# A fused attention and MLP kernel: work of its front end moved between ScalarE, VectorE and GpSimd, steps of two blocks at other places, one weight block fewer resident

## The chip, the cores and the metric

The kernel runs on one core of a Trainium2 chip. The core has a matrix engine (TensorE, PE in the profile), VectorE (DVE), ScalarE (ACT), GpSimd (POOL), SyncE (SP), which here only issues DMAs, and 16 DMA engines. The engines run side by side; each takes its own instructions in order and waits on semaphores for the others. On-chip data lies in SBUF, results of TensorE in eight banks of PSUM. The metric is the device time of one execution in microseconds, median over several runs. A profiled execution has a time and a trace of its own.

## The reference

Eight batches of 576 tokens go through attention with pooled keys and values (8 heads of 64), then through a Fourier mixing step, a layer norm and an MLP. The core of it:

```python
k_p = k.reshape(B, H, Sp, pool, D).mean(axis=3)        # Sp = 72, pool = 8
v_p = v.reshape(B, H, Sp, pool, D).mean(axis=3)
scores = scale * np.matmul(q, k_p.transpose(0, 1, 3, 2))
scores = scores - np.max(scores, axis=-1, keepdims=True)
attn = np.exp(scores)
attn = attn / (np.sum(attn, axis=-1, keepdims=True) + 1e-09)
x = np.matmul(attn, v_p)                # heads side by side: 8 x 576 x 512
...
mixed = np.real(fft(fft(x, axis=1), axis=2))
u = x + mixed
un = (u - mean(u)) / np.sqrt(var(u) + 1e-06)
out = u + np.maximum(un @ w_ch1, 0.0) @ w_ch2          # 512 -> 2048 -> 512
```

The factor on the scores is 1/8 for the head size, and the sum over 8 pooled keys needs another 1/8: together the 1/64 of the title's first part.

## The kernel before

**Split numbers.** TensorE multiplies numbers of type fp32r, which hold fewer bits than f32. Wherever accuracy is needed an operand is split into a high part (rounded to fp32r) and a low part (what is left), and a product becomes three: high by high, high by low, low by high. In names an h or "high" stands for the first, an l or "low" for the second. A high part is a cast, mostly on ScalarE; a low part is a subtraction, on VectorE or GpSimd.

**Two streams.** The MLP works on 9 blocks of 512 tokens (k = 0 to 8). Blocks 0 and 1 are plain: 12 matmuls of 128x512 make one tile of the hidden layer (line 875, tile g), and 12 more put it through the second weight matrix into four accumulators (line 839, tiles acc). Blocks 2 to 8 are the fast form: seven products of 128x256 (line 943, tile x) for a pair of tiles, joined by VectorE (adds L904, copy L947), a relu and a cast on ScalarE (L912, L913) and a subtraction on GpSimd (L914), and then the same line 839. Each block needs its tokens from a front end, fe(b) for batch b, which is made while the blocks before it run:

- scores of queries and pooled keys (psS, L422) with kpb, the pooled keys as written by the copies L360 and L361; row maxima; for b >= 2 a small VectorE multiplication of the maxima by 1/64 (L427); exp on ScalarE with scale 1/64 (L431); normalization on GpSimd (L439);
- V weights: sums over 8 on GpSimd (L352), the high part wh by ScalarE with a mask (L390), the low part wlo by VectorE (L391), for b >= 2; then transposes T, V and R of the attention (L459 to L483) and the product (psX, L507);
- the Fourier step: even and odd sums (tmpE L598, tmpO), their split (L591 on ScalarE, L592 on VectorE), and matmuls with cosine and sine tables (psA L631, psB L648, psQ and psP L665);
- means (psM), centring (L748), squares, variance (psVar, L792) and 1/sqrt; for b = 0 and 1 the result is spread over the partitions by a diagonal matrix dg (VectorE, L807 and L808) and a matmul into the same PSUM bank (L810); for b >= 2 the tokens X are multiplied by it in two halves of 128x1152, one on VectorE and one on GpSimd (L819), then split for the fast products (L723).

**Weights.** The two weight matrices arrive as 32 blocks of f64 (512 KB each). prep_w makes an f32 from each on ScalarE and VectorE (L191, L193, L195, L196), a high part on ScalarE (L203) and a low part on GpSimd (L205), and writes both to DRAM. The first ten are made before the first large matmul, beside the front end of batch 0; the others follow at every third step of blocks 0 and 1. RES lists the W2 high blocks that stay in SBUF; the others are read again for each block of tokens by SP's queue, nine tiles ahead (feed, LOOK).

**What sets the order.** fast() is a generator that yields after each group of matmuls; its count is the position pos. At each position, advance(pos) calls the next step of a front end if the tables say so: AT1 for fe(1), AT2 for fe(2), AT for the rest, each a list of positions, one per step. From position 92 on TensorE's order is as written; the other engines' order is left to a scheduler that simulates them, with VectorE's instructions of the fast products at high priority. issue_after holds an instruction behind a named one in that order (behind[...]). After block 0 four PSUM banks are shared by all tiles of front end and products; the other four are accumulators.

## Time and profile before

| quantity | value |
|---|---|
| median of 3 runs | 1103.25 us (1102.32 to 1977.59) |
| the profiled execution | 1107.79 us, of which the trace spans 1105.9 us |
| mean granted TensorE clock | 0.96 |
| ScalarE busy | 545.4 us (49%) |
| GpSimd busy | 543.6 us (49%) |
| instructions in the trace: TensorE, VectorE, ScalarE, GpSimd | 5974, 1442, 1607, 518 |
| largest DMA queue, share of 16 engines | 70.9% |
| TensorE's clock by slices of 27.6 us, the first ten, in tenths | 8 8 8 7 9 9 9 8 8 9 |

How it is read. A row names the source line, the engine, the operation and the program's tiles as out<-in. A wait in TensorE's list is idle time of TensorE, put down to the instruction that ended last before it could go on. A group's mean hides how it spreads, so where an engine's single instructions matter the timeline is read instead: start, duration, engine and line, with the idle time and its releaser in brackets behind. TensorE runs at a clock that the chip grants it, in tenths of full speed in the slices and as a number in the rows of a window; a low number means that the same matmuls take longer. The span is 1.9 us shorter than the time of the profiled execution, and that time is 4.5 us above the median.

### The profile page before, as it was taken

To read this page: it belongs to the slowest core of one execution; us is meant where nothing else is said; L and a number is where in the kernel's file an instruction comes from. 1 tells how busy PE (TensorE), PEld (TensorE's weight loads), DVE (VectorE), ACT (ScalarE), POOL (GpSimd) and SP (SyncE) were. 2 spreads that over 40 slices of the span, in tenths; PEclk is the share of its full clock that TensorE was granted. 3 is DMA by queue.
4 is the path that set the end of the run, shared out by engine and by line. 5 is a ranking of instruction groups with operands and counts; after the bars stand their busy time and mean duration, and the time that the engine had idled before them with its cause. 6 is when DMAs were issued, how large, how long until landed. Compare 5 with 4: busy or idle time off the path is not lost.

```text
span 1105.9 us, 18798 instructions
## 1 busy us (share of the span) xinstructions
PE 1017.3 (92%) x5974; PEld 878.2 (79%) x5974; DVE 747.4 (68%) x1442; ACT 545.4 (49%) x1607; POOL 543.6 (49%) x518
## 2 busy tenths in 40 slices
...
GB/s 297 230 188 347 274 318 262 208 220 262 207 141 127 196 223 209 211 262 220 197 227 194 255 207 224 222 243 223 206 191 235 198 197 243 306 256 254 302 253 144
DMA packets 160162, 253.75 MB, mean 229 GB/s; under 512 B 15808, under 2 KB 73152, under 8 KB 159808
## 3 DMA queue, kind: packets, MB, share of 16 engines
q1 hardware_dynamic: 159776, 249.88, 70.9%
q0 software_dynamic: 288, 2.66, 0.6%
q8 instruction: 49, 0.80, 0.3%
q14 instruction: 49, 0.40, 0.1%
...
## 4 chain that ended last, share of the span: by engine, by line
PE 64%; DVE 17%; DMA 6%; ACT 6%; issue 4%; POOL 3%; SPq 0%; DVEq 0%; ACTq 0%; POOLq 0%
PE acc L839 27%; PE x L943 20%; PE g L875 4%; PE psX L507 2%; PE psS L422 2%; PE psA L631 2%; DMA sx<-w1d 2%; PE psP L665 2%; PE psB L648 1%; DMA w1s<-sx 1%; DVE wlo L391 1%; DVE X L819 1%; DVE sx L904 1%; PE psQ L665 1%; DVE rw L400 1%
## 5 line engine op out<-in xcount | busy, mean ns | idle before, releaser
L914 POOL TENSOR_TENSOR hl<-sx,hh 128x512 fp32r<-128x512 f32 x112 | 151.7, 1354 | 217.7 <-ACT hh L913 198.0
L904 DVE TENSOR_TENSOR sx<-x,sx 128x256 f32<-128x256 f32 x336 | 155.3, 465 | 129.7 <-PE x L943 126.7
L943 PE MATMUL x<-un0h,w1op 128*128 128x256 f32 x896 | 176.0, 283 | 4.9 <-ACT U L510 1.5
L839 PE MATMUL acc<-hh,w2low 128*128 128x512 f32 x576 | 164.7, 399 | 0.0
L912 ACT ACTIVATE sx<-sx 128x512 f32<-128x512 f32 x112 | 71.2, 636 | 184.9 <-DVE sx L904 184.5
L943 PEld LDWEIGHTS x<-un0h,w1op 128*128 128x128 f32 x896 | 144.2, 191 | 16.5 <-DVE X L748 1.8
L943 PE MATMUL x<-un1h,w1op 128*128 128x256 f32 x672 | 134.0, 281 | 0.2
L943 PEld LDWEIGHTS x<-un1h,w1op 128*128 128x128 f32 x672 | 111.7, 189 | 13.4 <-DVE sx L904 1.5
L839 PEld LDWEIGHTS acc<-hh,w2low 128*128 128x128 f32 x576 | 101.6, 190 | 15.9
L839 PE MATMUL acc<-hh,w2high 128*128 128x512 f32 x324 | 98.3, 411 | 10.4 <-ACT hh L913 10.4
L839 PE MATMUL acc<-hl,w2high 128*128 128x512 f32 x324 | 94.5, 400 | 2.2 <-POOL hl L914 2.2
L943 PE MATMUL x<-un0l,w1op 128*128 128x256 f32 x448 | 88.8, 280 | 3.5 <-DVE un0l L723 3.5
L431 ACT ACTIVATE t<-psS,mx 128x72 f32<-128x72 f32 x240 | 73.5, 326 | 30.7 <-DVE mx L427 27.2
L439 POOL TENSOR_TENSOR t<-t,sm 128x720 f32<-128x720 f32 x30 | 45.8, 1526 | 64.0 <-DVE sm L438 47.5
L839 PEld LDWEIGHTS acc<-hh,w2high 128*128 128x128 f32 x324 | 58.8, 196 | 20.0 <-ACT hh L913 11.2
L839 PE MATMUL acc<-hl,w2h 128*128 128x512 f32 x252 | 72.2, 408 | 0.5 <-DVE hl L881 0.5
L943 PEld LDWEIGHTS x<-un0l,w1op 128*128 128x128 f32 x448 | 68.7, 190 | 3.7 <-DVE un0l L723 3.7
L913 ACT CAST hh<-sx 128x512 fp32r<-128x512 f32 x112 | 69.6, 621 | 2.9
L839 PE MATMUL acc<-hh,w2h 128*128 128x512 f32 x252 | 70.0, 398 | 1.0 <-DVE U L863 0.9
L839 PEld LDWEIGHTS acc<-hl,w2high 128*128 128x128 f32 x324 | 57.2, 189 | 12.2 <-POOL hl L914 3.2
L943 PE MATMUL x<-un1l,w1op 128*128 128x256 f32 x336 | 66.0, 278 | 0.0
L352 POOL TENSOR_TENSOR v<-v 128x256 f32<-128x256 f32 (+1 forms) x56 | 52.2, 931 | 26.1 <-DMA v<-in_vm 25.3
...
## 6 DMA issues: line engine op xcount, KB each, us to landing
...
w1op<-w1p SPq DMA_DIRECT2D x200, 256.0 KB, 3.6
w2low<-w2l SPq DMA_DIRECT2D x128, 256.0 KB, 3.4
...
```

The lines of the kernel that those rows point to most:

```text
L352: nc.gpsimd.tensor_tensor(out=out if n == 1 else src[:, :, 0:n], in0=src[:, :, 0] if n == 1 else src[:, :, 0:n], in1=src[:, :, 1] if n == ...
L422: nc.tensor.matmul(ps[:, c * W2J:(c + 1) * W2J], lhsT=q[:, r0:r0 + P], rhs=kpb[g % 2], start=True, stop=True)
L431: behind["S", b, gi, i] = nc.scalar.activation(t[:, c0 + c, h], pv[:, c, h], AF.Exp, scale=1.0 / 64.0, bias=mx[x], accum_out=sm[x])
L439: ins = nc.gpsimd.tensor_tensor(out=t, in0=t, in1=sm.unsqueeze(3).broadcast_to([P, 5, 2, J]), op=ALU.mult)
L665: nc.tensor.matmul(ps, lhsT=w, rhs=a, start=(i == 0), stop=(i == 6))
L839: nc.tensor.matmul(acc[e], lhsT=a[:, e], rhs=h, start=(f == 0 and x == 0), stop=(f == NFC - 1 and x == 2))
L875: nc.tensor.matmul(ps, lhsT=w[:, c], rhs=x[:, ti], start=(n == 0), stop=(n == 11))
L904: nc.vector.tensor_tensor(out=o, in0=x, in1=y, op=ALU.add)
L912: nc.scalar.activation(c, c, AF.Relu)
L913: nc.scalar.copy(out=h, in_=c)
L914: nc.gpsimd.tensor_tensor(out=l, in0=c, in1=raw(h), op=ALU.subtract)
L943: nc.tensor.matmul(ps, lhsT=w[:, q, i], rhs=y[:, c + i], start=(n == 0), stop=(n == 5))
```

## The change

Six edits and their tables:

1. K: the copies that write kpb multiply by 1/64; the multiplication of the maxima (L427) goes, and exp loses its scale.
2. V weights: ScalarE writes the masked f32 values to a new tile wf, casts it whole to wh, and GpSimd makes wlo by one subtraction of 128x128. The VectorE instructions L391 go (batches 0 and 1 are as before).
3. Tokens, b >= 2: four VectorE multiplications of 128x576 take the place of a VectorE and a GpSimd one of 128x1152.
4. Low weights: the subtraction L205 moves from GpSimd to VectorE for all 32 blocks.
5. Two splits in halves: L592 (b >= 2) and the centring L748 become two instructions each.
6. Order: the sign step L195 of weight blocks 0 to 3 is held behind the last low part of batch 0's psB (behind["Bv", 0]). AT1 and AT2 have other positions: AT2's come one or two earlier from its 18th entry on, AT1's last five 4 to 7 later or as they were. RES has six blocks where it had seven.

```diff
-RES = [0, 2, 5, 7, 9, 12, 14]
+RES = [0, 3, 6, 9, 11, 14]
...
-AT1 = [-1] * 7 + [2 + 3.5 * n for n in range(17)] + [93, 101, 106, 109, 112, 112, 112]
+AT1 = [-1] * 7 + [2 + 3.5 * n for n in range(17)] + [93, 101, 113, 116, 117, 117, 117]
...
-            nc.vector.tensor_scalar(out=dh[:, :, :, 1], in0=halves[:, :, :, 3], scalar1=0x8000, scalar2=None, op0=ALU.bitwise_and)
+            with tc.issue_after(behind["Bv", 0].ins) if n < 4 else ExitStack():
+                nc.vector.tensor_scalar(out=dh[:, :, :, 1], in0=halves[:, :, :, 3], scalar1=0x8000, scalar2=None, op0=ALU.bitwise_and)
...
-        nc.gpsimd.tensor_tensor(out=lw, in0=d0, in1=raw(wh), op=ALU.subtract)
+        nc.vector.tensor_tensor(out=lw, in0=d0, in1=raw(wh), op=ALU.subtract)
...
-                nc.scalar.copy(out=kb[0:64, 0:J], in_=ks[0:64])
-                nc.scalar.copy(out=kb[64:128, J:W2J], in_=ks[64:128])
+                nc.scalar.mul(kb[0:64, 0:J], ks[0:64], 1.0 / 64.0)
+                nc.scalar.mul(kb[64:128, J:W2J], ks[64:128], 1.0 / 64.0)
...
+            wf = wk.tile([P, P], F32, tag="wf", bufs=2, name="wf")
             for m, c, n, s0 in cols:
-                mm = mk[:, m:m + 1]
-                nc.scalar.mul(wh[:, c:c + n], vs[:, s0:s0 + n], mm)
-                nc.vector.scalar_tensor_tensor(out=wl[:, c:c + n], in0=vs[:, s0:s0 + n], scalar=mm, in1=raw(wh[:, c:c + n]), op0=ALU.mult, op1=ALU.subtract)
+                nc.scalar.mul(wf[:, c:c + n], vs[:, s0:s0 + n], mk[:, m:m + 1])
+            nc.scalar.copy(out=wh, in_=wf)
+            nc.gpsimd.tensor_tensor(out=wl, in0=wf, in1=raw(wh), op=ALU.subtract)
...
-                    nm = mx[:, c0:c0 + n]
-                    nc.vector.tensor_scalar(out=nm, in0=nm, scalar1=1.0 / 64.0, scalar2=None, op0=ALU.mult)
...
-                            behind["S", b, gi, i] = nc.scalar.activation(t[:, c0 + c, h], pv[:, c, h], AF.Exp, scale=1.0 / 64.0, bias=mx[x], accum_out=sm[x])
+                            behind["S", b, gi, i] = nc.scalar.activation(t[:, c0 + c, h], pv[:, c, h], AF.Exp, bias=mx[x], accum_out=sm[x])
...
-            eng.tensor_tensor(out=el, in0=src, in1=raw(eh), op=ALU.subtract)
+            for x in [slice(0, 2)] if b < 2 else [slice(0, 1), slice(1, 2)]:
+                eng.tensor_tensor(out=el[:, x], in0=src[:, x], in1=raw(eh[:, x]), op=ALU.subtract)
...
-            nc.vector.tensor_tensor(out=dst[0][:, n:2 * n], in0=ps, in1=raw(dst[0][:, 0:n]), op=ALU.subtract)
+            behind["Bv", b] = nc.vector.tensor_tensor(out=dst[0][:, n:2 * n], in0=ps, in1=raw(dst[0][:, 0:n]), op=ALU.subtract)
...
-            nc.vector.tensor_tensor(out=X[:, :, cl], in0=Ub[:, :, cl], in1=ps.unsqueeze(1).broadcast_to([P, 4, HS]), op=ALU.subtract)
+            for x in (0, 2):
+                nc.vector.tensor_tensor(out=X[:, x:x + 2, cl], in0=Ub[:, x:x + 2, cl], in1=ps.unsqueeze(1).broadcast_to([P, 2, HS]), op=ALU.subtract)
...
-            for e, x in ((nc.vector, slice(0, 2)), (nc.gpsimd, slice(2, 4))):
-                e.tensor_tensor(out=X[:, x], in0=X[:, x], in1=rn.unsqueeze(1).broadcast_to([P, 2, S]), op=ALU.mult)
+            for x in range(4):
+                nc.vector.tensor_tensor(out=X[:, x], in0=X[:, x], in1=rn, op=ALU.mult)
```

In the new file the lines stand one or two further down: L205 is L206, the cast to wh and GpSimd's subtraction are L392 and L393, L592 is L593, L748 L749, L810 L812, L819 L821, L839 L841, L875 L877, L904 L906, L913 L915, L947 L949.

By count, VectorE loses 60 L391, 48 L427 and the six old halves of L819, and gains 32 low weights, 24 token steps, 12 halves of L592 and 16 of L748. GpSimd loses 32 low weights and six token halves and gains 24 subtractions of 128x128. ScalarE gains 24 casts of 128x128. TensorE has the same matmuls. SP has eight more reads of a W2 block and one more write.

Three places of the order, before and after. First TensorE, in block 1, around the steps of fe(1) that AT1 places: the variance matmul L792 and the one that spreads 1/sqrt, L810, from the name psVar and the operand dg. Before:

```order
L792 MATMUL psVar_2097<-avg,lf 128x1 x5
L875 MATMUL g_1_2_2118<-un0h_869,w1op 128x512 x4
L875 MATMUL g_1_2_2118<-un0l_870,w1op 128x512 x4
L875 MATMUL g_1_2_2118<-un0h_869,w1op 128x512 x4
L839 MATMUL acc_0_2072<-hh,w2h 128x512
...
L839 MATMUL acc_3_2075<-hh,w2low 128x512
L810 MATMUL psVar_2097<-dg,avg 128x288 x2
```

After, the rows that end at the same matmul, now L812:

```order
L841 MATMUL acc_2_2076<-hl,w2high 128x512
L841 MATMUL acc_3_2077<-hl,w2high 128x512
L877 MATMUL g_1_3_2203<-un0h_871,w1op 128x512 x4
L471 MATMUL psV_0_2208<-ident,t_3_1881 128x128
L471 MATMUL psV_0_2208<-ident,t_2_1970 128x128
L472 MATMUL psV_0_2208<-ident,rt 32x128
L877 MATMUL g_1_3_2203<-un0l_872,w1op 128x512 x4
L483 MATMUL psR_0_2224<-ident,rt 32x128 x4
L877 MATMUL g_1_3_2203<-un0h_871,w1op 128x512 x4
L812 MATMUL psVar_2099<-dg,avg 128x288 x2
L424 MATMUL psS_0_0_2253<-kpb_78,q_0_2046 128x144 x3
```

L810 came 20 large matmuls behind L792 (rows of the two are left out above); L812 comes 48 behind, with transposes of fe(2) (psT, psV, psR) ahead of it too.

Second VectorE, in a block from the third on, at the token scaling (X<-X,rb) and the copy L947 that TensorE's products need (sx<-x). Before:

```order
L464 TENSOR_TENSOR al<-psT_2_6152,ah 128x512
L786 SCALAR_TENSOR_TENSOR nt<-nt,lf 128x576
L904 TENSOR_TENSOR sx<-x,sx 128x256
L478 TENSOR_TENSOR al<-psV_0_6190,ah 128x64
L787 SCALAR_TENSOR_TENSOR rb<-nt,lf 128x576
L478 TENSOR_TENSOR al<-psV_0_6190,ah 128x64
L819 TENSOR_TENSOR X<-X,rb 128x1152
L947 COPY sx<-x 128x256
L491 TENSOR_TENSOR R<-psR_0_6204,R 32x512
L491 TENSOR_TENSOR R<-psV_0_6190,R 32x64
```

After:

```order
L464 TENSOR_TENSOR al<-psT_2_6160,ah 128x512
L788 SCALAR_TENSOR_TENSOR nt<-nt,lf 128x576
L906 TENSOR_TENSOR sx<-x,sx 128x256
L478 TENSOR_TENSOR al<-psV_0_6196,ah 128x64
L789 SCALAR_TENSOR_TENSOR rb<-nt,lf 128x576
L478 TENSOR_TENSOR al<-psV_0_6196,ah 128x64
L821 TENSOR_TENSOR X<-X,rb 128x576 x2
L949 COPY sx<-x 128x256
L821 TENSOR_TENSOR X<-X,rb 128x576 x2
L491 TENSOR_TENSOR R<-psR_0_6210,R 32x512
L491 TENSOR_TENSOR R<-psV_0_6196,R 32x64
```

The copy stood behind one step of 128x1152 and stands behind two of 128x576, with two more after it.

Third VectorE, in a later batch, at the V weights (wlo, rw) and the sums and split of the Fourier step (tmpE, f), with the adds of the fast products (sx<-x) between them. Before:

```order
L391 SCALAR_TENSOR_TENSOR wlo<-vs,mk,wh 128x64
L904 TENSOR_TENSOR sx<-x,sx 128x256
L518 TENSOR_TENSOR U_85<-psX_1_5296,U_85 128x288
L598 TENSOR_TENSOR tmpE<-U_85 128x2x287
L391 SCALAR_TENSOR_TENSOR wlo<-vs,mk,wh 128x63
L391 SCALAR_TENSOR_TENSOR wlo<-vs,mk,wh 128x1
L400 SCALAR_TENSOR_TENSOR rw_81<-vt,mk,rw_81 32x63
L400 SCALAR_TENSOR_TENSOR rw_81<-vt,mk,rw_81 32x1
L904 TENSOR_TENSOR sx<-x,sx 128x256
L592 TENSOR_TENSOR f<-tmpE,f 128x580
L904 TENSOR_TENSOR sx<-x,sx 128x256
L904 TENSOR_TENSOR sx<-x,sx 128x512
```

After:

```order
L517 TENSOR_TENSOR U_85<-psX_1_5302,U_85 128x288
L518 TENSOR_TENSOR U_85<-psX_1_5302,U_85 128x288
L906 TENSOR_TENSOR sx<-x,sx 128x256
L599 TENSOR_TENSOR tmpE<-U_85 128x2x287
L402 SCALAR_TENSOR_TENSOR rw_81<-vt,mk,rw_81 32x63
L402 SCALAR_TENSOR_TENSOR rw_81<-vt,mk,rw_81 32x1
L609 TENSOR_TENSOR xe<-xt,xe 1x290
L906 TENSOR_TENSOR sx<-x,sx 128x256
L593 TENSOR_TENSOR f<-tmpE,f 128x290 x2
L906 TENSOR_TENSOR sx<-x,sx 128x256
L906 TENSOR_TENSOR sx<-x,sx 128x512
```

The three rows of wlo are gone, and the split of f is two halves, which stand together.

6 lines of the change are left out of this document (3 added, 3 removed).

## The prediction

> **What bounds the kernel now.** I read the page's first part and its chain, then TensorE's own waits, then the timelines around the longest of those waits, then windows for the granted clock.
>
> ```profile
> PE 1017.3 (92%) x5974; PEld 878.2 (79%) x5974; DVE 747.4 (68%) x1442; ACT 545.4 (49%) x1607; POOL 543.6 (49%) x518
> PE 64%; DVE 17%; DMA 6%; ACT 6%; issue 4%; POOL 3%; SPq 0%; DVEq 0%; ACTq 0%; POOLq 0%
> ```
>
> TensorE is busy for 1017.3 of 1105.9 us and holds 64% of the chain; VectorE holds 17% of it at 68% busy. Both programs have the same count of matmuls, so the change can only win what TensorE idles (88.6 us) and what it loses at a lower clock. The waits say who ends that idle time (us in total, times, longest):
>
> ```profile
> PE acc L839 <- ACT hh L913: 10.4, 4, 2.7
> PE psS L422 <- DVE sx L947: 9.9, 4, 2.5
> PE psVar L810 <- DVE dg L807: 7.8, 2, 6.7
> PE psA L631 <- DVE f L592: 4.1, 1, 4.1
> PE x L943 <- DVE un0l L723: 3.5, 1, 3.5
> ```
>
> Two waits of about 2.5 us come four times each, all from 340 us on; one of 6.7 us comes once. First the rows ahead of one "psS <- L947" wait (start, duration, engine):
>
> ```profile
> 345.75 1.36 DVE L819 TENSOR_TENSOR X<-X,rb 128x1152 f32<-128x1152 f32 x1
> ...
> 578.84 2.66 POOL L819 TENSOR_TENSOR X<-X,rb 128x1152 f32<-128x1152 f32 x1 [1.82 <-ACT ah L476]
> 578.97 3.75 DVE L819 TENSOR_TENSOR X<-X,rb 128x1152 f32<-128x1152 f32 x1
> 582.64 0.41 DVE L947 COPY sx<-x 128x256 f32<-128x256 f32 x1
> 583.10 1.81 PE L422 MATMUL psS<-kpb,q 128*128 128x144 f32 x6 [2.46 <-DVE sx L947]
> ```
>
> VectorE's half of the token scaling takes 1.36 us at 345.75 and 3.75 us at 578.97, where GpSimd's half has started just before it: it ends 1.2 us after GpSimd's 2.66 us are over. The copy L947 stands behind it, and TensorE idles 2.46 us for that copy. Now the same ahead of an "acc <- hh" wait:
>
> ```profile
> 504.59 1.95 DVE L391 SCALAR_TENSOR_TENSOR wlo<-vs,mk,wh 128x64 fp32r<-128x64 f32 x2
> 511.27 1.81 POOL L610 TENSOR_TENSOR tmpO<-U 128x576 f32<-128x576 f32 x1 [3.21 <-DVE U L518]
> 511.71 2.44 DVE L391 SCALAR_TENSOR_TENSOR wlo<-vs,mk,wh 128x63 fp32r<-128x63 f32 x2
> 514.96 2.38 DVE L592 TENSOR_TENSOR f<-tmpE,f 128x580 fp32r<-128x580 f32 x1
> 517.27 1.54 DVE L904 TENSOR_TENSOR sx<-x,sx 128x256 f32<-128x256 f32 x3
> 519.04 2.08 PE L839 MATMUL acc<-hh,w2high 128*128 128x512 f32 x4 [2.68 <-ACT hh L913]
> L391 DVE SCALAR_TENSOR_TENSOR wlo<-vs,mk,wh x60: 204/285/2089, 139.4 to 846.6; 128x64 fp32r<-128x64 f32 x36, 128x63 fp32r<-128x63 f32 x12, 128x1 fp32r<-128x1 f32 x12
> ```
>
> The low parts of the V weights (L391) take a median of 0.285 us, yet here two cost 1.95 and two 2.44 us, the second pair beside GpSimd's L610. VectorE falls behind, its three L904 come at once at 517.27, ScalarE's relu after them, and TensorE idles 2.68 us. Both kinds of wait come from VectorE instructions that read two SBUF tensors and are held while GpSimd works.
>
> The Trainium skill says the same ("SBUF — State Buffer", Who interferes with whom): such an instruction contends with a GpSimd instruction that reads SBUF, and whichever comes first keeps the shared port to its end. The rule speaks against two parts of this change, which put more such instructions on VectorE; what it would make of the time is the first rival.
>
> **The change, part by part.** The sum is made against the profiled execution, 1107.79 us with a span of 1105.9, which is 4.5 above the median of 1103.25; the gains are taken off the median.
>
> *Tokens in four VectorE steps.* GpSimd loses six instructions of 2.66 us or more. VectorE gets 24 of half the old size, about half of 1.36 = 0.7 us each, and the order puts the copy L947 after the second of four. TensorE stopped at 583.10 - 2.46 = 580.64, having just made what L947 copies; two steps from 578.97 on end at 580.4, so the copy is late no more, unless GpSimd's L914 (1.35 us mean, quoted below) gets in between. Of the 9.9 us I take 9. Steps of 0.7 us beside L914 the trace does not show; ends 0 and 9.9, nearest the free 1.36.
>
> *V weights.* L391's 60 instructions leave VectorE: ahead of the late L904 that is 1.95 + 2.44 = 4.4 us, more than the 2.68 that TensorE waits. In their place come 24 copies on ScalarE and 24 subtractions of 128x128 on GpSimd. The row of that size below gives 0.71 us each, 17 us in all, on an engine that is 49% busy and loses the token scaling and the low weights; hidden, but they hold the port in turn. L592 (2.38 here) is cut in two, which helps only if L904 gets between, and the order leaves both halves together. Of the 10.4 us I take 9; ends 4 (L592 still held) and 10.4.
>
> ```profile
> L352 POOL TENSOR_TENSOR v<-v 128x128 f32<-128x128 f32 x28 | 20.0, 713 | 0.9
> L914 POOL TENSOR_TENSOR hl<-sx,hh 128x512 fp32r<-128x512 f32 x112 | 151.7, 1354 | 217.7 <-ACT hh L913 198.0 <-DVE U L863 10.7 <-ACT ah L476 7.1
> 519.00:523.00 4.00, 3.96 (x14) 3.57 (x15) 0.14 (x1) 1.98 (x5) 3.93 (x5) 0.50 0.47 162
> 583.00:587.00 4.00, 3.90 (x16) 3.71 (x17) 3.26 (x9) 0.90 (x3) 1.58 (x2) 0.57 0.01 3
> 754.00:758.00 4.00, 4.00 (x18) 3.62 (x19) 0.20 (x1) 1.75 (x5) 2.90 (x4) 0.60 0.38 123
> ```
>
> *The clock after those waits.* In a window's row the granted clock stands ahead of the DMA share. Behind two of the "hh" waits it is 0.50 and 0.60 for 4 us, behind one "psS" wait 0.57. Lost: 3.96 x 0.50 + 4.00 x 0.40 + 3.90 x 0.43 = 5.3 us; I take 5 back, ends 0 and 8 (another 0.40 for each wait not quoted that is like these).
>
> The Trainium skill ("TensorE: Matmul & The Clock Gate", Part 1) lets the clock fall after at least one idle window of about 3.4 us; by that no wait of 2.7 us would cost clock, and the result would be 5 us higher, 1075. The trace has 0.50 right behind 2.68 us, so the term stays.
>
> *Steps of block 1's front end (AT1).* The 6.7-us wait:
>
> ```profile
> 222.03 1.17 PE L792 MATMUL psVar<-avg,lf 128*128 128x1 f32 x10
> 227.67 1.10 PE L839 MATMUL acc<-hh,w2low 128*128 128x512 f32 x4
> 235.36 0.25 DVE L808 TENSOR_SCALAR dg<-ident,yy 128x64 f32<-128x64 f32 x1
> 235.50 1.33 PE L810 MATMUL psVar<-dg,avg 128*128 128x288 f32 x2 [6.73 <-DVE dg L807]
> 235.00:240.00 5.00, 4.01 (x8) 2.55 (x9) 0.61 (x2) 0.80 (x2) 0.84 (x1) 0.50 0.52 175
> ```
>
> TensorE is done with L839 at 228.8, and L810's operand dg is written at 235.6. The new order has 28 more large matmuls and the T, V and R transposes ahead of L810: 28 x 0.24 (1.10 for four, which overlap at the ends) = 6.7 us, and some 2 us of transposes. So L810 is reached at about 237 and finds dg ready. Gone are 6.73 us and, at a clock of 0.50 in 235 to 240, 2.0 us more. I take 9; ends 5 and 11. The cost: its PSUM bank is held from 222 to about 239, with three banks left to the rest; no row prices that, so it bounds the low end.
>
> *Steps of block 2 (AT2).* They come 8 large matmuls earlier (1.9 us) and lose some L427 on the way; the wait of 3.5 us for un0l, at the seam to the third block, shrinks by that and by its clock. I take 3, ends 0 and 5.
>
> *K scaled at the copy.* This row has its price (ns: least, median, most):
>
> ```profile
> L427 DVE TENSOR_SCALAR mx<-mx x48: 155/172/1362, 207.3 to 825.8; 128x6 f32<-128x6 f32 x24, 128x4 f32<-128x4 f32 x24
> 44.45 0.66 ACT L591 CAST f<-tmpE 128x580 fp32r<-128x580 f32 x1
> 42.81 4.17 DVE L195 TENSOR_SCALAR wdl<-U 128x512 uint16<-128x512 uint16 x1
> 49.48 1.61 DVE L592 TENSOR_TENSOR f<-tmpE,f 128x580 fp32r<-128x580 f32 x1
> 82.48 3.78 PE L875 MATMUL g<-un0h,un1h 128*128 128x512 f32 x8 [5.51 <-ACT un0h L711]
> L195 DVE TENSOR_SCALAR wdh<-U x8: 432/462/1034, 59.1 to 157.8; 128x512 uint16<-128x512 uint16 x8
> L196 DVE SCALAR_TENSOR_TENSOR wdh<-sx,wdh x8: 674/1098/2032, 40.8 to 165.8; 128x512 int32<-128x512 int32 x8
> L205 POOL TENSOR_TENSOR w1low<-wdh,un1h x9: 1271/1296/1737, 61.5 to 166.8; 128x512 fp32r<-128x512 f32 x9
> 75.00:175.00 100.00, 92.83 (x388) 69.92 (x387) 85.21 (x124) 70.47 (x157) 70.86 (x64) 0.90 0.88 307
> 75.00:100.00 25.00, 19.49 (x52) 12.51 (x51) 23.83 (x36) 21.57 (x50) 19.28 (x16) 0.60 0.92 313
> 125.00:150.00 25.00, 25.00 (x104) 18.22 (x103) 22.60 (x34) 19.09 (x44) 12.68 (x12) 1.00 0.98 350
> ```
>
> The 48 L427 of 0.17 us go; ScalarE's copies become activations of the same size. Hidden beside TensorE's matmuls except where the terms above already count them: nothing more.
>
> *Block 0.* The other rows are for this and the next part. L195 of one weight block sat on VectorE for 4.17 us from 42.81, ahead of L592, whose other operand ScalarE's L591 had ready at 45.1; TensorE waited 4.1 us for it. In the new order the L195 of the first four weight blocks stand behind block 0's last B part, so L592 can start at 45.1 instead of 49.48: 4.4 us. But the four pairs L195 and L196, 4 x (0.46 + 0.67) = 4.5 us free of holds, and three low subtractions, 3 x 0.67 = 2.0, now come between B and block 0's means, where one pair of 1.1 stood: 5.4 more, of which I take half, 2.7, as hidden while VectorE waits for TensorE. That leaves 1.7 gained. Between those means and the centring (L748), seven L195 and L196 lose a hold of 1.10 - 0.67 = 0.43 each, since no L205 runs on GpSimd beside them, and one low subtraction of 0.67 is added: 2.3 more. What the first large matmul at 82.48 gains beyond that is not priced. I take 4; ends 0 and 7.
>
> *Low weights.* 32 subtractions move from GpSimd (1.30 us) to VectorE, where L196 of the same size takes 0.67 free and 1.10 at the median of its row. About 25 fall in 75 to 175 us, where VectorE is busy for 85.2 and has 14.8 left: 25 x 1.10 = 27.5, which is 12.7 too many. Against that L195 and L196 lose their holds by L205, and TensorE is fed ten weight blocks ahead. Price between 0 and 12.7; I take 6.
>
> *One W2 block fewer resident.* SP issues eight more reads of 256 KB and one more write, among 925 issues; the DMA share in the windows from 519 on is 0.01 to 0.47 (the last number but one), and the reads are issued nine tiles ahead. Nothing.
>
> Sum: 9 + 9 + 5 + 9 + 3 + 4 - 6 = 33 us gained, 1103 - 33 = **1070 us**.
>
> **The rivals.**
>
> *The hold moves along (0.12).* Each of the 24 steps, and both halves of L592, can be held by one L914 or L352. Two steps ahead of L947, held 1.35 us each, are 2.7 us: as long as today's wait. Then the token term is 0, the V term 4 and the clock term 1: 1070 + 9 + 5 + 4 = 1088. The skill's rule would give this at its worst. Against it: today's 3.75 needed a partner of 2.66, and L914 is half as long.
>
> *VectorE is the bound from 75 to 175 us (0.09).* If none of its idle time there can be used, all 27.5 us reach TensorE instead of 6: 1070 + 21 = 1091. For it: 23.83 of 25 us busy in 75 to 100. Against it: TensorE is full in 125 to 150 with VectorE at 22.60.
>
> *Slower than before (0.07).* The low V weights now queue on GpSimd, in order, behind L352 and L914, and TensorE's V matmuls need them. With 24 groups the change breaks even at 33 / 24 = 1.4 us of wait for each, and is slower by over 2% from 55 / 24 = 2.3 us on (1125). For it: one L914 and one L352 ahead are 1.35 + 0.71 = 2.1 us. Against it: that wait must come at TensorE every time, and GpSimd is idle half the time.
>
> **Chances.** The forecast, 1055 to 1081, has 0.66, and a still faster end 0.06. The range of 1055 to 1091 adds the first two rivals less a little at its edge and leaves out the slower one: 0.8. Two per cent, 22 us, is about what a measurement of this kernel can tell from no change, and puts the line at 1081: faster 0.72, same 0.21, slower 0.07.
>
> **What the profile would show.** Right: TensorE's waits for L947 and L913 (L949 and L915 in the new file) under 1 us each; its wait for dg (L809 there) under 1 us; token steps (L821) near 0.7 us; the first large matmul near 78 us; a granted clock near 1.0 from 200 us on. Wrong: L821 or L593 at 1.5 us and more with the old waits behind them (first rival); TensorE idle between 90 and 200 us for low weights (second); TensorE waiting for wlo (third). What I could not price, the bank held by psVar and the reordered first 90 us, would make it wrong without any of these.

## The result, and the profile after

| | before | changed |
|---|---|---|
| median | 1103.90 us of 4 runs (1102.32 to 1977.59) | 1077.37 us of 4 runs (1076.58 to 1079.97) |
| ratio, 95% interval | | 0.9768 (0.9745 to 0.9792) |
| span of the profiled execution | 1105.9 us | 1074.8 us |

One of the four executions of before took 1977.59 us; the ratio leaves it out, and without it the median of before is 1103.25. The change makes the kernel 26.5 us faster, 2.3% by the ratio; between the two profiled executions it is 31.1 us. The forecast was 1070 us, in a range of 1055 to 1091.

The page of the changed kernel, engines and chain (busy us, share of the span; then shares of the chain that ended last):

```profile
PE 1009.0 (94%) x5974; PEld 872.7 (81%) x5974; DVE 720.9 (67%) x1412; ACT 552.1 (51%) x1631; POOL 494.7 (46%) x504
PE 69%; DVE 14%; DMA 6%; ACT 4%; issue 3%; POOL 3%; SPq 1%; DVEq 0%; POOLq 0%; ACTq 0%
```

TensorE is busy for 8.3 us less with as many matmuls, at a mean granted clock of 0.975 where it was 0.960, and the idle share fell by two points. VectorE's share of the chain went from 17% to 14%. Who ends TensorE's idle time now (us in total, times, longest):

```profile
PE x L945 <- issue: 8.7, 4, 2.2
PE psA L632 <- DVE f L593: 7.9, 2, 5.5
...
PE g L877 <- ACT un0h L712: 4.7, 2, 4.5
...
PE psM L743 <- DVE s L695: 3.7, 1, 3.7
PE psB L649 <- DVE f L593: 3.3, 3, 2.1
PE x L945 <- DVE un0l L724: 3.0, 1, 3.0
...
PE acc L841 <- ACT hh L915: 2.1, 4, 1.0
...
PE psVar L812 <- ACT rb L813: 0.8, 1, 0.8
```

The wait for hh went from 10.4 to 2.1 us and the one for dg is gone (0.8 us for rb is left there). The wait for the copy L947 is gone too, but at the top stands a wait of 8.7 us in four times that the kernel before did not have, f costs 7.9 + 3.3 us where it cost 4.1 + 1.0, and at 64 us there is one of 3.7 us for the means of batch 0 (psM), where before the longest for psM was 0.7. So three waits went and three came in.

Because both programs issue the large matmuls in the same order, the start of the n-th of them can be set against its start before. The changed kernel is ahead by (us; read off the two traces):

| at matmul | time before | ahead by | what lies there |
|---|---|---|---|
| 1st | 82.5 | 4.6 | batch 0's front end |
| 121st | 127.5 | 8.9 | first weight blocks, dg of batch 0 |
| 361st | 198.2 | 9.1 | rest of block 0 |
| 541st | 278.4 | 19.4 | dg of batch 1 |
| 601st | 300.3 | 10.3 | f of batch 2: 9.2 lost again |
| 961st | 407.6 | 21.7 | seam to the third block |
| 2821st | 820.3 | 33.4 | four later blocks |
| last | 1100.8 | 31.2 | last block: 2.2 lost |

**Where the token steps' gain went.** The timeline of the changed kernel at one of the four places (start, duration, engine, line):

```profile
551.49 1.42 DVE L821 TENSOR_TENSOR X<-X,rb 128x576 f32<-128x576 f32 x2
...
552.82 0.42 DVE L949 COPY sx<-x 128x256 f32<-128x256 f32 x1
...
553.15 1.88 POOL L916 TENSOR_TENSOR hl<-sx,hh 128x512 fp32r<-128x512 f32 x1 [3.61 <-ACT hh L915]
553.16 2.49 DVE L821 TENSOR_TENSOR X<-X,rb 128x576 f32<-128x576 f32 x2
...
553.29 1.00 PE L424 MATMUL psS<-kpb,q 128*128 128x144 f32 x6
555.68 0.68 DVE L491 TENSOR_TENSOR R<-psR,R 32x512 fp32r<-32x512 f32 x1
...
556.46 0.47 PE L945 MATMUL x<-un0h,w1op 128*128 128x256 f32 x2 [2.16 <-issue]
```

The copy L949 is early, as forecast: it stands behind two steps of 0.7 us. But steps three and four follow it, here 2.49 us together: the third takes 0.75 us and the fourth, beside GpSimd's L916, 1.82. Behind them stands L491, the subtraction that reads psR. TensorE starts L945 0.1 us after that subtraction ends at 556.36. "issue" means that the profile shows no releaser; the reading as a wait for psR's PSUM bank was tested (e2).

The wait costs more than its 2.2 us, because behind three of the four TensorE's granted clock (the number ahead of the DMA share) is at 0.50 for 3.4 us; behind the first, at 445.8 us, it stays at 1.00. Here are two of the three windows; the third, from 669.9 us on, reads 0.51:

```profile
557.30:560.70 3.40, 3.40 (x14) 3.02 (x14) 2.47 (x7) 2.05 (x13) 0.12 (x1) 0.50 0.39 102
782.60:786.00 3.40, 3.37 (x12) 3.01 (x13) 2.53 (x8) 2.19 (x13) 0.38 (x1) 0.50 0.16 28
```

That is 3 x 3.4 x 0.5 = 5.1 us of lost clock, by this reckoning 13.8 us for the four waits in all.

### The profile page after: what moved, and what is told of

The parts are those of the page before. It is cut to its first block, busy times and chain, and to the rows that moved or that the text cites. A ratio compares the mean times of both kernels' runs of the same rounds, so it can differ in the third digit from the quotient of the medians.

```text
span 1074.8 us, 18778 instructions
## 1 busy us (share of the span) xinstructions
PE 1009.0 (94%) x5974; PEld 872.7 (81%) x5974; DVE 720.9 (67%) x1412; ACT 552.1 (51%) x1631; POOL 494.7 (46%) x504
## 4 chain that ended last, share of the span: by engine, by line
PE 69%; DVE 14%; DMA 6%; ACT 4%; issue 3%; POOL 3%; SPq 1%; DVEq 0%; POOLq 0%; ACTq 0%
PE acc L841 29%; PE x L945 21%; PE g L877 5%; PE psS L424 3%; PE psX L507 3%; PE psP L666 2%; PE psB L649 2%; DVE sx L906 1%; PE psQ L666 1%; DMA v<-in_vm 1%; PE psT L459 1%; DMA sx<-w1d 1%; DVE f L593 1%; DMA out<-U 1%; PE psA L632 1%
## 5 line engine op out<-in xcount | busy, mean ns | idle before, releaser
L916 POOL TENSOR_TENSOR hl<-sx,hh 128x512 fp32r<-128x512 f32 x112 | 149.5, 1335 | 225.2 <-ACT hh L915 209.8
L906 DVE TENSOR_TENSOR sx<-x,sx 128x256 f32<-128x256 f32 x336 | 154.7, 465 | 139.2 <-PE x L945 136.1
L945 PE MATMUL x<-un0h,w1op 128*128 128x256 f32 x896 | 175.7, 284 | 10.3 <-issue 8.7
L841 PE MATMUL acc<-hh,w2low 128*128 128x512 f32 x576 | 166.6, 403 | 0.0
L945 PEld LDWEIGHTS x<-un0h,w1op 128*128 128x128 f32 x896 | 143.8, 190 | 21.8 <-issue 9.4
L945 PE MATMUL x<-un1h,w1op 128*128 128x256 f32 x672 | 134.4, 282 | 0.0
L945 PEld LDWEIGHTS x<-un1h,w1op 128*128 128x128 f32 x672 | 112.4, 190 | 12.2
L841 PEld LDWEIGHTS acc<-hh,w2low 128*128 128x128 f32 x576 | 102.6, 191 | 16.0
L841 PE MATMUL acc<-hh,w2high 128*128 128x512 f32 x360 | 104.8, 401 | 2.1 <-ACT hh L915 2.1
L841 PE MATMUL acc<-hl,w2high 128*128 128x512 f32 x360 | 103.6, 397 | 0.1
L945 PE MATMUL x<-un0l,w1op 128*128 128x256 f32 x448 | 89.3, 281 | 3.0 <-DVE un0l L724 3.0
L431 ACT ACTIVATE t<-psS,mx 128x72 f32<-128x72 f32 x240 | 73.6, 328 | 21.9 <-DVE mx L426 21.5
L353 POOL TENSOR_TENSOR v<-v 128x256 f32<-128x256 f32 (+1 forms) x56 | 53.6, 957 | 55.4 <-DMA v<-in_vm 54.2
L841 PEld LDWEIGHTS acc<-hh,w2high 128*128 128x128 f32 x360 | 63.6, 190 | 12.4 <-ACT hh L915 2.9
L841 PEld LDWEIGHTS acc<-hl,w2high 128*128 128x128 f32 x360 | 63.1, 189 | 10.3 <-POOL hl L916 0.9
L945 PEld LDWEIGHTS x<-un0l,w1op 128*128 128x128 f32 x448 | 68.9, 190 | 3.2 <-DVE un0l L724 3.2
L915 ACT CAST hh<-sx 128x512 fp32r<-128x512 f32 x112 | 69.5, 620 | 3.0
L945 PE MATMUL x<-un1l,w1op 128*128 128x256 f32 x336 | 66.4, 279 | 0.0
L841 PE MATMUL acc<-hh,w2h 128*128 128x512 f32 x216 | 61.1, 400 | 1.7 <-DVE U L865 1.7
L724 POOL TENSOR_TENSOR un1l<-X,un1h 128x256 fp32r<-128x256 f32 (+11 forms) x26 | 31.3, 1204 | 65.5 <-ACT un1h L723 43.4
L841 PE MATMUL acc<-hl,w2h 128*128 128x512 f32 x216 | 59.9, 398 | 0.0
```

The costliest lines, as they stand in the source:

```text
L353: nc.gpsimd.tensor_tensor(out=out if n == 1 else src[:, :, 0:n], in0=src[:, :, 0] if n == 1 else src[:, :, 0:n], in1=src[:, :, 1] if n == ...
L431: behind["S", b, gi, i] = nc.scalar.activation(t[:, c0 + c, h], pv[:, c, h], AF.Exp, bias=mx[x], accum_out=sm[x])
L841: nc.tensor.matmul(acc[e], lhsT=a[:, e], rhs=h, start=(f == 0 and x == 0), stop=(f == NFC - 1 and x == 2))
L906: nc.vector.tensor_tensor(out=o, in0=x, in1=y, op=ALU.add)
L915: nc.scalar.copy(out=h, in_=c)
L916: nc.gpsimd.tensor_tensor(out=l, in0=c, in1=raw(h), op=ALU.subtract)
```

## The experiments

Each kernel is the changed one with the edit shown. The kernel before ran beside each on the same chip; its median was 1104.62 us beside e1 to e4, 1105.49 beside e5 to e8 and 1106.98 beside e9 to e12. Ratios are to it.

| kernel | median us | ratio (95% interval) | against the changed kernel: median, us | the same by the ratios, us |
|---|---|---|---|---|
| e1 old AT2 | 1077.34 | 0.9754 (0.9705 to 0.9804) | 0.0 | -1.5 |
| e2 R first | 1071.50 | 0.9705 (0.9655 to 0.9756) | -5.9 | -7.0 |
| e3 low weights on GpSimd | 1089.15 | 0.9867 (0.9806 to 0.9927) | +11.8 | +10.9 |
| e4 V weights on VectorE | 1085.45 | 0.9821 (0.9772 to 0.9870) | +8.1 | +5.9 |
| e5 old token scaling | 1076.16 | 0.9736 (0.9689 to 0.9783) | -1.2 | -3.5 |
| e6 old AT1 | 1086.30 | 0.9828 (0.9781 to 0.9876) | +8.9 | +6.6 |
| e7 no hold behind psB | 1085.80 | 0.9822 (0.9771 to 0.9872) | +8.4 | +6.0 |
| e8 R first, V weights of batch 2 on VectorE | 1071.71 | 0.9693 (0.9655 to 0.9731) | -5.7 | -8.3 |
| e9 R first, f ahead of the combination | 1071.22 | 0.9677 (0.9632 to 0.9722) | -6.2 | -10.0 |
| e10 block 0 as before (e3 and e7) | 1090.74 | 0.9852 (0.9799 to 0.9906) | +13.4 | +9.3 |
| e11 whole splits | 1084.09 | 0.9785 (0.9737 to 0.9833) | +6.7 | +1.9 |
| e12 old K scale | 1082.78 | 0.9782 (0.9734 to 0.9830) | +5.4 | +1.5 |

The medians are set against 1077.37 us, the ratios against 0.9768, times 1104 us. The medians of before differ by up to 3 us between the sessions, and each ratio is uncertain by about 5 us, so differences of a few us are read from the traces and not from this table alone; only e2, e3, e6, e8, e9 and e10 stand more than 6 us off by the ratios.

### e1: the old AT2

```diff
-AT2 = [-6, 2, 4, 6, 8, 17, 18, 21, 22, 23, 24, 26, 27, 28, 29, 30, 31, 33, 34, 37, 38, 41, 42, 43, 44, 44,
-       53, 54, 56, 57, 59, 60, 61, 61, 62, 64, 65, 66, 69, 70, 70, 79, 80, 80, 80, 81, 81, 100]
+AT2 = [-6, 2, 4, 6, 8, 17, 18, 21, 22, 23, 24, 26, 27, 28, 29, 30, 31, 34, 35, 38, 39, 43, 44, 45, 46, 46,
+       55, 56, 58, 59, 61, 62, 63, 63, 64, 66, 67, 68, 71, 72, 72, 81, 82, 82, 82, 83, 83, 100]
```

> The changed kernel with the old AT2 (fe(2)'s steps one or two positions later). In the changed kernel's trace TensorE waits 5.5 us at 273 and 2.1 us at 285 for the split f (L593) of batch 2, which the kernel before did not. Theory A: the earlier steps bring TensorE to psA before VectorE can have f, beside the combination of weights (L226 to L229), whose positions did not move; with the old steps both waits fall under 1 us and the time to 1069 to 1072 us. Rival B: the two halves of L593 are held by GpSimd (3.87 us for two) wherever they stand; a wait of 4 to 5 us stays near 290 us, and since un0l at the seam comes later, the time is 1077 to 1080.

Neither came out as put. The wait for f of batch 2 fell under 1 us, as theory A had it, but the time stayed. Another wait took its place (waits and timeline of e1):

```profile
PE psS L424 <- ACT kpb L361: 15.3, 4, 8.4
...
270.22 0.45 DVE L609 TENSOR_TENSOR xe<-xt,xe 1x290 fp32r<-1x290 f32 x1
...
270.70 0.33 SPq L332 DMA_DIRECT2D k<-in_kt  x1
...
281.26 1.81 PE L424 MATMUL psS<-kpb,q 128*128 128x144 f32 x6 [8.38 <-ACT kpb L361]
```

TensorE waits 8.4 us for the pooled keys of batch 3. The tile of k is also that of xt, so the load of k (270.70) can only start once L609 has read xt (270.22 + 0.45), and in this order L609 stands behind f; GpSimd's sums follow, with others between. So the chain of f and the chain of k compete for the same stretch, and AT2 chooses which is late.

### e2: the subtraction that reads psR ahead of the last two token steps

```diff
-      40, 41, 44, 46, 48, 49, 52, 52, 53, 55, 57, 59, 65, 66, 66, 79, 80, 80, 81, 82, 82, 104]
+      40, 41, 44, 46, 48, 49, 52, 52, 53, 55, 57, 59, 65, 66, 66, 79, 80, 80, 81, 82, 91, 104]
...
-                nc.vector.tensor_tensor(out=R[32:64, a0:a1], in0=src, in1=raw(R[0:32, a0:a1]), op=ALU.subtract)
+                behind["Rv", b, gi] = nc.vector.tensor_tensor(out=R[32:64, a0:a1], in0=src, in1=raw(R[0:32, a0:a1]), op=ALU.subtract)
...
-                nc.vector.tensor_tensor(out=X[:, x], in0=X[:, x], in1=rn, op=ALU.mult)
+                with (tc.issue_after(behind["Rv", b + 1, 0].ins) if x > 1 and b > 2 and b + 1 < B else ExitStack()): nc.vector.tensor_tensor(out=X[:, x], in0=X[:, x], in1=rn, op=ALU.mult)
```

> The changed kernel with the third and fourth token step (L821) behind the subtraction L491 that reads psR, for batches 3 to 6; for that the step with L821 is issued at position 91 where it was 82. Theory A: the four waits of 2.2 us that the profile puts down to 'issue' at 446, 557, 670 and 783 are for the PSUM bank of psR, which L491 lets go only behind four token steps; they fall under 0.5 us each, 8.7 - 2 = 7 us or more, 1068 to 1070 us. Rival B: they are time of TensorE's instruction stream and not of that bank; they stay at 2.2 us and the time at 1077. Rival C: the operands un0h and un0l of the next block come too late by the nine positions, TensorE waits for L723 or L724 at the seams at 445 + 113 n, and the time is 1077 or more although the four waits are gone.

The same place in e2's timeline:

```profile
553.58 1.42 DVE L821 TENSOR_TENSOR X<-X,rb 128x576 f32<-128x576 f32 x2
...
554.92 0.42 DVE L949 COPY sx<-x 128x256 f32<-128x256 f32 x1
...
555.37 0.68 DVE L491 TENSOR_TENSOR R<-psR,R 32x512 fp32r<-32x512 f32 x1
555.39 1.00 PE L424 MATMUL psS<-kpb,q 128*128 128x144 f32 x6
556.08 1.07 DVE L821 TENSOR_TENSOR X<-X,rb 128x576 f32<-128x576 f32 x1
...
556.15 0.48 PE L945 MATMUL x<-un0h,w1op 128*128 128x256 f32 x2
```

L491 ends at 556.05, L945 starts at 556.15, and TensorE does not idle between L424 and L945. All four waits are gone, so A holds: the "issue" wait was for psR's bank. Set against the changed kernel, the four places give 2.0, 3.6, 3.7 and 3.6 us, the wait alone at the first and wait and clock at the others. Of these 12.9 us 5.9 reach the time: 2.0 are lost near 395 us, and behind three of the places TensorE now waits for GpSimd's L916, 4.1 us in total. At 1071.5 us, in four runs from 1070.0 to 1075.3, this version beats both kernels.

### e3, e7, e10: the low weights and the order of block 0

e3 moves L206 back to GpSimd, e7 takes the hold off L196, e10 does both:

```diff
-        nc.vector.tensor_tensor(out=lw, in0=d0, in1=raw(wh), op=ALU.subtract)
+        nc.gpsimd.tensor_tensor(out=lw, in0=d0, in1=raw(wh), op=ALU.subtract)
```

```diff
-            with tc.issue_after(behind["Bv", 0].ins) if n < 4 else ExitStack():
+            with ExitStack():
```

> The changed kernel with the low weights (L206) on GpSimd again, all else as changed. The prediction had their move to VectorE as a cost of 6 us (0 to 12.7): then this kernel takes 1071 us. Rival: since the changed kernel's first large matmul comes 4.6 us earlier and the next 120 of them gain 4.3 us more, the move is a gain, by L195 and L196 that are held no longer: then this kernel takes 1080 to 1086, with the first large matmul near 82 us and L196 back at a median of 1.1 us.

> The changed kernel without the hold of the first four L196 (sign step of weight blocks) behind block 0's psB. The prediction took 1.7 us for it within 4: the psA wait for f near 47 us grows from 2.4 to 4 us or more, and the time is 1078 to 1080 us. Rival: the weights are ready sooner without it, since the first large matmul is bound by VectorE's work from 55 us on; the first large matmul starts earlier than 77.9 and the time is 1074 to 1077 us.

> The changed kernel with both the low weights on GpSimd and no hold of the first sign steps: the start as in the kernel before. e3 alone cost 12 us at the median (4.3 in its profiled execution), e7 alone 8.4. If the two are gains of different places, they add: 1090 to 1098 us, and the large matmuls from the 240th on stand 11 us or more behind the changed kernel's. If each needs the other (the hold piles work on VectorE that pays only when GpSimd does not hold it), the sum is what the two traces of before and after show there, 8.9 us: 1084 to 1088.

The low weights' move is a gain and not a cost of 6. The rows of L206 in the changed kernel and in e3 (least, median, most, in ns):

```profile
L206 DVE TENSOR_TENSOR w1low<-wdh,un1h x9: 677/684/1599, 61.3 to 157.8; 128x512 fp32r<-128x512 f32 x9
L206 DVE TENSOR_TENSOR w2low<-wdl,w2high x10: 624/900/1292, 66.2 to 165.3; 128x512 fp32r<-128x512 f32 x10
```

```profile
L206 POOL TENSOR_TENSOR w1low<-wdh,un1h x9: 1257/1283/1747, 59.6 to 172.4; 128x512 fp32r<-128x512 f32 x9
L206 POOL TENSOR_TENSOR w2low<-wdl,w2high x10: 1272/1383/1847, 63.3 to 176.3; 128x512 fp32r<-128x512 f32 x10
PE acc L841 <- DVE hl L883: 2.8, 1, 2.8
```

By the medians VectorE does in 0.68 to 0.90 us what takes GpSimd 1.28 to 1.38, so a weight block can be ready sooner. Not as either text had it: in e3 the first large matmul starts at 78.5 and not at 82 us. The loss comes in the 120 matmuls after it, with 5.2 us, among them 2.8 us of TensorE's wait for hl, which VectorE delivers late. Of e3's four runs one, the profiled one, took 1080.9 us, the others 1087 to 1091, so its 11.8 us are not all explained by that trace (4.3 us).

Taking away the hold (e7) costs 5.3 us already at the first large matmul. Its timeline at block 0's f, with the changed kernel's behind it:

```profile
48.80 1.43 DVE L197 SCALAR_TENSOR_TENSOR wdl<-U,wdl 128x512 int32<-128x512 int32 x1
50.15 1.60 DVE L593 TENSOR_TENSOR f<-tmpE,f 128x580 fp32r<-128x580 f32 x1
51.80 1.23 PE L632 MATMUL psA<-ca,f 128*128 128x258 f32 x4 [4.08 <-DVE f L593]
```

```profile
46.57 1.70 PE L632 MATMUL psA<-ca,f 128*128 128x258 f32 x12 [2.36 <-DVE f L593]
```

The weight's L197 goes first in e7 and TensorE gets f 5.2 us later. The theory was right on that wait and too low on the time; the four runs of e7 lie between 1081.2 and 1090.3 us, and this trace is of the slowest. Together (e10) the two cost 13.4 us by the medians, less than 11.8 + 8.4 = 20.2, and 9.3 by the ratios, less than 16.9. But at the 241st large matmul e3 stands 4.9 us behind the changed kernel, e7 6.7 and e10 10.0, which is nearly the sum. The time lies in the range put for gains that add, and the 10.0 us lie between the 8.9 and the 11 put for the two readings, so these were not told apart.

### e4: the low V weights on VectorE

```diff
-            wf = wk.tile([P, P], F32, tag="wf", bufs=2, name="wf")
...
-                nc.scalar.mul(wf[:, c:c + n], vs[:, s0:s0 + n], mk[:, m:m + 1])
-            nc.scalar.copy(out=wh, in_=wf)
-            nc.gpsimd.tensor_tensor(out=wl, in0=wf, in1=raw(wh), op=ALU.subtract)
+                mm = mk[:, m:m + 1]
+                nc.scalar.mul(wh[:, c:c + n], vs[:, s0:s0 + n], mm)
+                nc.vector.scalar_tensor_tensor(out=wl[:, c:c + n], in0=vs[:, s0:s0 + n], scalar=mm, in1=raw(wh[:, c:c + n]), op0=ALU.mult, op1=ALU.subtract)
```

> The changed kernel with the low V weights formed by VectorE again (60 L391), all else as changed. The prediction's theory: L391 held by GpSimd makes VectorE late, TensorE waits about 2.6 us four times for hh again and loses clock behind it; 1085 to 1090 us. Rival: with the token halves and the low weights gone from GpSimd the L391 are held seldom, those waits stay under 1 us, and the time is 1075 to 1080.

The prediction's theory holds: 1085.45 us, and in e4's waits and windows (PEclk is the number ahead of the DMA share):

```profile
PE acc L841 <- ACT hh L915: 10.9, 4, 2.7
...
497.30:501.30 4.00, 4.00 (x17) 3.69 (x18) 0.50 (x2) 1.97 (x5) 4.00 (x5) 0.57 0.33 106
612.20:616.20 4.00, 3.95 (x29) 3.78 (x30) 0.90 (x3) 2.38 (x6) 3.93 (x5) 1.00 0.51 146
```

Four waits of 2.7 us for hh are back. The windows stand behind two of them: the clock is 0.57 behind the one and 1.00 behind the other. At 290 us e4 is 5.3 us ahead of the changed kernel: 3.1 of them it has already at 252 us, the rest comes where f is less late (a wait of 2.1 us and not 5.5). It falls behind only in the later blocks, by 14.2 us to the end.

### e5: tokens scaled as before

```diff
-            for x in range(4):
-                nc.vector.tensor_tensor(out=X[:, x], in0=X[:, x], in1=rn, op=ALU.mult)
+            for e, x in ((nc.vector, slice(0, 2)), (nc.gpsimd, slice(2, 4))):
+                e.tensor_tensor(out=X[:, x], in0=X[:, x], in1=rn.unsqueeze(1).broadcast_to([P, 2, S]), op=ALU.mult)
```

> The changed kernel with the tokens scaled as before: a half of 128x1152 on VectorE and one on GpSimd. The prediction took 9 us for the four steps: then this kernel takes 1086 us. Theory after the runs so far: the copy's wait of 2.46 us was only replaced by a wait of 2.2 us for psR's bank at the same four places, so going back costs 1 us there and at most 2 us of clock; 1077 to 1080 us, with the waits psS for L949 back at 2.4 us and those called 'issue' gone.

```profile
PE psS L424 <- DVE sx L949: 9.9, 4, 2.5
```

The old wait is back in full, 9.9 us in four, the 8.7 us of "issue" are gone, and the time is not longer (1076.16). The clock is at 0.50 behind two of the four, for 6.4 us, so wait and lost clock come to 13.1 us, against 13.8 in the changed kernel. Up to the last block the two traces are 0.5 us apart; e5 gains 2.2 us more there (last section). So the four steps by themselves gained nothing.

### e6: the old AT1

```diff
-AT1 = [-1] * 7 + [2 + 3.5 * n for n in range(17)] + [93, 101, 113, 116, 117, 117, 117]
+AT1 = [-1] * 7 + [2 + 3.5 * n for n in range(17)] + [93, 101, 106, 109, 112, 112, 112]
```

> The changed kernel with the old AT1 (steps of fe(1)). The prediction took 9 us for the later positions: TensorE waits 6 to 7 us for dg before psVar again, and loses 2 us of clock behind it; 1084 to 1088 us. Rival: the waits of 5.5 and 2.1 us for f at 273 and 285 come because TensorE arrives there 12 us earlier than it did; they shrink by what the dg wait takes, and the time is 1077 to 1080 us.

```profile
PE psVar L812 <- DVE dg L809: 6.6, 1, 6.6
```

(The last five entries of the new AT1 are 5 to 7 positions later than the old.) The wait is back with 6.6 us and the time is 1086.3, 8.9 more by the medians and 6.6 by the ratios. The rival fell in its sum: the waits for f shrink (psA from 7.9 to 2.4 us), but one of 4.5 us for R (L491) comes in.

### e8 and e9: what delays f of batch 2

Both start from e2. e8 leaves the V weights of batch 2 on VectorE; e9 holds the seventh and eighth combination of weights behind batch 2's f:

```diff
-                nc.scalar.mul(wf[:, c:c + n], vs[:, s0:s0 + n], mk[:, m:m + 1])
-            nc.scalar.copy(out=wh, in_=wf)
-            nc.gpsimd.tensor_tensor(out=wl, in0=wf, in1=raw(wh), op=ALU.subtract)
+                nc.scalar.mul(wf[:, c:c + n] if b > 2 else wh[:, c:c + n], vs[:, s0:s0 + n], mk[:, m:m + 1])
+                if b <= 2: nc.vector.scalar_tensor_tensor(out=wl[:, c:c + n], in0=vs[:, s0:s0 + n], scalar=mk[:, m:m + 1], in1=raw(wh[:, c:c + n]), op0=ALU.mult, op1=ALU.subtract)
+            if b > 2: nc.scalar.copy(out=wh, in_=wf); nc.gpsimd.tensor_tensor(out=wl, in0=wf, in1=raw(wh), op=ALU.subtract)
```

```diff
-                eng.tensor_tensor(out=el[:, x], in0=src[:, x], in1=raw(eh[:, x]), op=ALU.subtract)
+                behind["F", b, n] = eng.tensor_tensor(out=el[:, x], in0=src[:, x], in1=raw(eh[:, x]), op=ALU.subtract)
...
-        nc.vector.tensor_tensor(out=a22, in0=a21, in1=a22, op=ALU.add)
+        with (tc.issue_after(behind["F", 2, 290].ins) if j > 5 else ExitStack()): nc.vector.tensor_tensor(out=a22, in0=a21, in1=a22, op=ALU.add)
```

> The kernel of e2_r_first with, besides, the low V weights of batch 2 alone on VectorE as before; batches 3 to 7 keep ScalarE and GpSimd. e4 was 5.3 us ahead of the changed kernel at 290 us and behind it only later. Theory: the V weights of batch 2 are what delays f and tmpE at 260 to 290 us (GpSimd busy beside the combination of weights), and their price there is 4 to 5 us, while the gain lies in batches 3 to 7; 1066 to 1068 us. Rival: the 5.3 us of e4 come from another order of block 0 and 1 on VectorE and not from those weights; the waits for f stay at 5 and 2 us, 1070 to 1073 us.

> The kernel of e2_r_first with, besides, the seventh and eighth combination of weights (L226 to L229 on VectorE, L233 on GpSimd) behind batch 2's first split f (L593). Theory: the waits of 6.3 and 2.3 us for f near 274 and 285 us are VectorE's, which runs the held L228, L229 and then the held halves of L593; with the combination behind f the first wait falls to 1 to 2 us and the second under 1.5, and the time to 1065 to 1067 us. Rival: the halves of L593 are held by GpSimd's sums (L353) and not by anything of the combination, so f comes late anyway, or kpb becomes what TensorE waits for, as in e1; 1070 to 1073 us.

e8 brings nothing: waits of 4.0 and 3.6 us for f stay at 270 and 283 us, as its rival had it. First the changed kernel's timeline at that place, then e9's:

```profile
268.39 1.40 DVE L229 TENSOR_TENSOR sx<-sx 128x256 f32<-128x256 f32 x1
...
269.72 3.87 DVE L593 TENSOR_TENSOR f<-tmpE,f 128x290 fp32r<-128x290 f32 x2
269.93 0.78 POOL L353 TENSOR_TENSOR k<-k 128x288 f32<-128x288 f32 x1
...
270.68 1.25 POOL L233 TENSOR_TENSOR sx<-sx 128x512 f32<-128x512 f32 x1
...
273.27 1.39 PE L632 MATMUL psA<-ca,f 128*128 128x258 f32 x4 [5.50 <-DVE f L593]
```

```profile
266.03 3.73 DVE L593 TENSOR_TENSOR f<-tmpE,f 128x290 fp32r<-128x290 f32 x2
...
269.81 0.63 PE L632 MATMUL psA<-ca,f 128*128 128x258 f32 x3 [1.55 <-DVE f L593]
...
285.32 0.43 DVE L226 TENSOR_TENSOR sx<-sx 128x256 f32<-128x256 f32 x1 [7.76 <-DMA sx<-w1d]
285.78 0.48 DVE L638 SCALAR_TENSOR_TENSOR AB<-AB,mk,psA 2x258 fp32r<-2x258 f32 x1
...
286.41 1.30 PE L424 MATMUL psS<-kpb,q 128*128 128x144 f32 x4 [8.08 <-DVE AB L638]
```

Two halves of L593, 0.45 us each where they are free, take 3.87 us in a row of GpSimd's L353 and L233, and 3.73 us in e9, where no L233 runs. So a hold of that length does not need L233, but the start of f is the combination's: with that out of the way f ends 3.8 us sooner than in the changed kernel (4.4 sooner than in e2) and the wait falls from 6.3 us in e2 to 1.6, as the theory said. Then a worse one comes: the last L226 waits 7.8 us for its load of w1d, and everything behind it on VectorE waits with it, among it L638, for which TensorE idles 8.1 us. The time is the same, 1071.22. Theory right on f, wrong on the time; in these three experiments (e1, e8, e9) the stretch from about 260 to 290 us keeps its length, whichever chain is moved: from the 541st large matmul to the 601st it takes 31.1 us in the changed kernel, 31.8, 32.2 and 31.1 in the three, and took 21.9 before. Where TensorE comes to it later, it is shorter: e6 and e12 stand 15.4 and 7.9 us behind the changed kernel at the 541st and need 21.7 and 22.3 us, so that they are 6.1 us behind and 0.8 ahead at the 601st. Much of what other parts gain ahead of 260 us is waited off here. What it would take to shorten it is open.

### e11 and e12: the halves and K's scale

```diff
-            for x in [slice(0, 2)] if b < 2 else [slice(0, 1), slice(1, 2)]:
-                eng.tensor_tensor(out=el[:, x], in0=src[:, x], in1=raw(eh[:, x]), op=ALU.subtract)
+            eng.tensor_tensor(out=el, in0=src, in1=raw(eh), op=ALU.subtract)
...
-            for x in (0, 2):
-                nc.vector.tensor_tensor(out=X[:, x:x + 2, cl], in0=Ub[:, x:x + 2, cl], in1=ps.unsqueeze(1).broadcast_to([P, 2, HS]), op=ALU.subtract)
+            nc.vector.tensor_tensor(out=X[:, :, cl], in0=Ub[:, :, cl], in1=ps.unsqueeze(1).broadcast_to([P, 4, HS]), op=ALU.subtract)
```

```diff
-                nc.scalar.mul(kb[0:64, 0:J], ks[0:64], 1.0 / 64.0)
+                nc.scalar.copy(out=kb[0:64, 0:J], in_=ks[0:64])
...
+                    nc.vector.tensor_scalar(out=mx[:, c0:c0 + n], in0=mx[:, c0:c0 + n], scalar1=1.0 / 64.0, scalar2=None, op0=ALU.mult)
...
-                            behind["S", b, gi, i] = nc.scalar.activation(t[:, c0 + c, h], pv[:, c, h], AF.Exp, bias=mx[x], accum_out=sm[x])
+                            behind["S", b, gi, i] = nc.scalar.activation(t[:, c0 + c, h], pv[:, c, h], AF.Exp, scale=1.0 / 64.0, bias=mx[x], accum_out=sm[x])
...
```

> The changed kernel with L593 and L749 whole again (one instruction of 128x580 and one of 128x1152). The prediction gave the halves nothing of their own, since they stand together: 1077 us, within 2. Rival: half an instruction is held half as long and the adds L906 get between, so whole ones cost; L593 rises from 0.9 us for two to 2 us, waits for f grow in later batches, and the time is 1080 to 1084.

> The changed kernel with the factor 1/64 taken out of kpb again: the 48 multiplications of the maxima on VectorE and the scale of exp are back. The prediction gave this part nothing: 1077 us, within 2. Rival: 48 x 0.17 = 8 us on VectorE, each ahead of an exp that TensorE's next psS needs, show up for a quarter to a half of them: 1079 to 1082 us.

Both came out longer at the median, 1084.09 and 1082.78 us, but by the ratios they stand only 0.0017 and 0.0014 from the changed kernel (2 us), within the intervals. The traces say where: e11's is 1.3 us behind at the first large matmul, 6.1 at the 121st, with a new wait of 2.1 us for batch 0's squares in between, and 8.7 at the end. Of the two, only L749's halves apply to that batch; whether they are the cause, or another order that the scheduler made of block 0, was not told apart. The row of the whole L592 (ns) shows that the later batches did not need its halves:

```profile
L592 DVE TENSOR_TENSOR f<-tmpE,f x7: 752/754/3798, 43.5 to 837.4; 128x580 fp32r<-128x580 f32 x7
```

Its median is 0.75 us, where before the change it was 2.38; what held it went away with L391 (in e4, with L391 back, the first half of L593 takes 2.08 us in four batches). e12's trace is 4.8 us behind at 240 us and 7.9 at 264, 2.8 ahead at 361, 0.6 behind at 517 and 5.0 at the end, with the 48 small multiplications back at their old median:

```profile
L428 DVE TENSOR_SCALAR mx<-mx x48: 152/170/1360, 197.9 to 797.3; 128x6 f32<-128x6 f32 x24, 128x4 f32<-128x4 f32 x24
```

One W2 block fewer resident, and the two halves apart from each other, were not tried.

## Why the prediction was right

The time lies in the range, and the direction and the size are as forecast, 26.5 us for 33 (31.2 between the two traces, from the first of which the terms were read). But the terms behind it were partly wrong, and their errors cancelled: that the sum came out so near is in part luck. "Measured" is what undoing the part alone costs, by the medians and then by the ratios; the parts overlap, so these columns add to more than the whole.

| step | predicted gain | measured, medians | by the ratios | verdict |
|---|---|---|---|---|
| tokens in four steps | 9 | -1 (e5) | -3 | wrong: the wait moved to psR's bank |
| V weights | 9, and part of 5 for the clock | 8 (e4) | 6 | mechanism right; size 14 in the later blocks, 5 lost earlier |
| AT1 | 9 | 9 (e6) | 7 | mechanism right, size in part luck |
| AT2 | 3 | 0 (e1) | -1 | wrong: kpb against f |
| block 0 and low weights | 4 - 6 = -2 | 13 (e10) | 9 | wrong in sign |
| K's scale | 0 | 5 (e12) | 2 | hidden cost not priced, size open |
| halves | 0 | 7 (e11) | 2 | size and place open |

*Tokens.* The copy is indeed "late no more", and yet that was worth nothing; the step that failed is that the end of the copy's wait is a gain. The prediction looked for what was late behind the copy and not for what stands behind the steps on VectorE. L491 was behind the token step before as well (583.08 in the timeline of before, 0.44 us after the copy began); by our reading it cost nothing only because TensorE was waiting for the copy at that time. The first rival's price (token term 0) came true by another mechanism than its own, of which the hold of step four (1.82 us for 0.75) is a part.

*V weights.* Four waits for hh from 10.4 to 2.1 us, and back to 10.9 in e4. From 290 us to the end e4 loses 14.2 us, which is what the 9 and the clock were meant for. But it comes to 290 us 5.3 us ahead of the changed kernel, a cost that the prediction did not have; e8, with batch 2's V weights alone on VectorE, does not get it back, so its cause stays open. GpSimd's new subtraction takes a median of 0.46 us and not 0.71. The rival that GpSimd's queue would be late with wlo did not come: the trace has no wait of TensorE for GpSimd's wlo.

*AT1.* Predicted 9 from 6.73 us of wait and 2 of clock. In the traces the part is worth 15.4 us at the 541st large matmul, 6.1 at the 601st, where the waits for f take the rest, and 8.5 at the end: the net is near the 9 put, the way to it is not the one put. No wait of TensorE names the bank held longer by psVar, but no run tested it.

*AT2.* The part was priced by the seam's wait for un0l, which did shrink (3.5 to 3.0, and 3.9 in e1). What it brought nearer, TensorE at psA before VectorE is there with f (5.5 and 2.1 us), had no row before and was not looked for.

*Block 0 and low weights.* The estimate counted VectorE's load ("12.7 too many") and took half of that as a cost. What it left out is the way through: a weight block needs L195, L196, then the low part, and on GpSimd that last step took 1.3 us behind other GpSimd work, while one of the four kinds of L197 on VectorE went from a median of 0.69 to 1.56 us (e3; the others stay within 0.2). That this chain, and not the load, is what counts is argued from these rows and not shown by a run of its own. The second rival (VectorE as the bound from 75 to 175 us) is refuted by the windows of the changed kernel, in which TensorE is full at 100 to 125 us with VectorE at 21.56, and stays full to 175 us:

```profile
75.00:100.00 25.00, 21.11 (x80) 14.67 (x81) 24.40 (x46) 22.54 (x53) 12.01 (x12) 0.86 0.86 280
100.00:125.00 25.00, 25.00 (x114) 19.64 (x112) 21.56 (x43) 20.17 (x48) 9.01 (x11) 1.00 1.03 375
```

In 75 to 100 us the granted clock is 0.86, where it was 0.60, and in e10's same window, in which its first large matmul comes 2.9 us later, it is low again:

```profile
75.00:100.00 25.00, 20.09 (x51) 12.36 (x52) 23.20 (x38) 21.07 (x46) 17.74 (x16) 0.59 0.97 322
```

So a part of the gain at the start is clock, which the prediction had looked for only behind the later waits.

*Clock.* The prediction gave 5 us for the clock behind the waits for L947 and hh, argued from 0.50 behind 2.68 us, against the page "TensorE: Matmul & The Clock Gate" of the Trainium skill (Part 1), by which an idle window of about 3.4 us is needed. Waits of 2.7 us went both ways here: 0.57 behind one and 1.00 behind another in e4. So shorter waits than the page's window can cost clock, and the trace's 0.50 was no rule either: of the eight such waits before, four paid, 16.2 us at 0.50 in all, or 8.1 us lost; of the changed kernel's four "issue" waits of 2.2 us three paid, 5.1 us. So about 3 of the 5 us came back.

The prediction's signs came out so: waits for L949 and hh are at most 1.0 us each; the first large matmul starts at 77.9 us (near 78); the granted clock is 0.99 from 200 to 1070 us, where it was 0.97; the token steps take 0.75 us at the median, with some near 1.9 (L821's row, in ns):

```profile
L821 DVE TENSOR_TENSOR X<-X,rb x24: 746/751/1857, 330.0 to 890.8; 128x576 f32<-128x576 f32 x24
```
